# One pool of six places for x and the weight blocks, and a last product stored by quarters

## The chip, the cores and the metric

The kernel runs on one core of one Trainium2 chip. The metric is the device time of one execution in microseconds (us); shown is the median of three runs. A core has five engines that work side by side, each through its own instruction queue in order: PE (TensorE, matrix products; PEld is its loading of weights), DVE (VectorE), ACT (ScalarE), POOL (GpSimd) and SP (SyncE, which here only issues DMA transfers). Products end up in PSUM, eight banks of 128 partitions by 512 float32 values; everything else lies in SBUF or in DRAM.

## The reference, cut to what matters

```
kv  = einsum('bhsd,bhse->bhde', k, v)            # 8 batches, 8 heads, 576 rows, 64 features
o   = einsum('bhsd,bhde->bhse', q, kv)
x   = o / sqrt(mean(o*o, -1) + 1e-6) * g_norm    # laid out as 4608 tokens x 512
h   = x @ w_in                                    # 512 x 2048
g   = max(h, 0)**2
out = g @ w_out                                   # 2048 x 512, all float32
```

## The kernel before, in words

**Strips.** The 4608 tokens are 36 tiles of 128; four tiles make a strip, so there are nine strips, 0 to 8. Per strip the kernel does the "up" products (x times `w_in`), squares the positive part into four quarters `gt`, then does the "down" products (`gt` times `w_out`). Attention for the next strip is cut into small slices (`slices`, L675 to L740) that are put between the steps of the current strip.

**Products by Strassen's scheme.** A product of 2 by 2 blocks is made of seven block products, numbered 1 to 7 in the code (`p`). Strip 0 uses plain products up and one level of the scheme down. Strip 1 uses one level up and two levels down. Strips 2 to 8 use two levels both ways: each block product p is again seven small products, called j. In `small_products` (L1043) one j is four matmuls in the code and eight PE instructions in the profile. `together` (L1058) adds the small products of one p from PSUM into an output tile: one ACT copy and five DVE additions.

**Weight blocks.** The weights of one deep down product come as two blocks: block (s, p, 0) is 768 KB from `w_out` and holds j = 3, 1, 2; block (s, p, 1) is 1024 KB from `w_deep` and holds j = 5, 6, 7, 4. A deep up product takes one 768 KB block from `w_in_deep`. All are asked for in one fixed order (`to_stream`, L912) by calls of `stream` (L921). Such a call takes a place in a pool and issues a DMA on SP; if the place is still being read, the DMA instruction waits on SP, and all that is queued on SP behind it waits too. The pool ("stream", L1345) has four places of 8 KB per partition. In strips 0 and 1 the same places also hold tiles of computed weights: `w_t` (sums of `w_out` blocks, made on DVE and stored to `w_deep`) and `w_i` (sums of `w_in`, made on POOL in `deep_sums_in`, L1146, and stored to `w_in_deep`).

**x.** A strip's x, transposed, lies in a tile `xT` of 8 KB per partition, in a pool of its own with two places (L86). It is opened by the first of `open_xt` (L622). Tiles 0 to 8 are transposed on PE and copied in by ACT (`first_features`, `features`). Later tiles are transposed on DVE (`squares_x`), stored to DRAM (`send_x`, L646) and read back by four DMAs of 64 KB (`fetch_x`, L651). The read-back is asked for when a planner's clock, which adds 2.2 per up step of strip 1 and 3.2 per down step, has gone on by 18 for tiles 9 to 11, or by 6 for later tiles.

**Order around the change.** Strip 1 has 28 up steps (i = 0 to 27), then 14 down steps: k = 0 to 6 through `DEEP_ORDER` = (4, 1, 2, 6, 5, 7, 3), each in two halves i = 0, 1. At each up step i of strip 1 one slice of attention is done, slice i - 1 of the list from L702 on. Blocks are asked for at up steps 17, 20, 21 and 23, and then by `down_deep` (L1084) after the products of each half, up to k = 6, i = 0. In strips 2 to 8, k = 0 has no products of i = 0 left (they are done among the up steps), and i = 1 asks for two.

**The last product.** In strip 8 the last product is p = 3 (k = 6). Its j come in three groups, (1), (2, 6, 5, 7), (4, 3), and `together` does one part of the sums after each; the last part ends with one DMA of 256 KB (`send`, L946). Products 5 and 3 share their PSUM banks: 3 adds on top of 5.

Of the kernel before, what the change touches and what calls it, by code (L numbers as in the profile page):

```python
# [10 lines left out]
FP32 = mybir.dt.float32  # L11
# [4 lines left out]
ALU = mybir.AluOpType  # L16
# [4 lines left out]
def kernel(  # L21
# [35 lines left out]
    P = 128  # L57
# [25 lines left out]
    rest_pool = ctx.enter_context(tc.tile_pool(name="rest", bufs=1))  # L83
    qt_pool = ctx.enter_context(tc.tile_pool(name="qt", bufs=NP + 1))
    xn_pool = ctx.enter_context(tc.tile_pool(name="xn", bufs=3))
    xt_pool = ctx.enter_context(tc.tile_pool(name="xt", bufs=2))  # L86
    small = ctx.enter_context(tc.tile_pool(name="small", bufs=3))
    g_pool = ctx.enter_context(tc.tile_pool(name="g", bufs=4))
    dram = ctx.enter_context(tc.tile_pool(name="dram", bufs=1, space=bass.MemoryType.DRAM))
    c_pool = ctx.enter_context(tc.tile_pool(name="c", bufs=6))  # L90
    conv = ExitStack()
    raw_pool = conv.enter_context(tc.tile_pool(name="raw", bufs=8))
    spare_pool = conv.enter_context(tc.tile_pool(name="spare", bufs=1))
    wtmp = conv.enter_context(tc.tile_pool(name="wtmp", bufs=4))
# [526 lines left out]

    def open_xt(s):  # L622
        if s not in xt:
            xt[s] = xt_pool.tile([P, STRIP // SQ, NP, SQ], FP32, name="xT", tag="xT")
        return xt[s]

    def features(n):
# [18 lines left out]
    def send_x(n):  # L646
        d = sent[n] = dram.tile([P, 4, NP, SQ], FP32, name="x_d", tag="x_d", bufs=2 * NT)
        nc.sync.dma_start(out=d, in_=squared.pop(n))
        tiles_due.append((clock[0] + (6 if n >= DEEP_UP * NT + NT else 18), fetch_x, (n,)))

    def fetch_x(n):  # L651
        s, i = divmod(n, NT)
# [47 lines left out]
    ready[1] = len(slices)  # L700
    T, K, last = transposed_query, key_value, query_pairs(1)[2]
    slices += [(query_means, (last,)), (K, (2, 0, 1)), (T, (2, 0)), (roots_normalized, (last,)), (T, (2, 1))]  # L702
    slices += [(T, (2, 2)), (features, (last[0],)), (T, (2, 3)), (K, (2, 2, 3))]
    pair_ends = []
    for b in range(2, B):
        pairs = query_pairs(b)
# [93 lines left out]
    def out_rows(n):  # L800

        to = []
        for t in range(2):
            m, c = divmod(n + t, PAIR)
            b, c_b = (2 * m, c) if c < C else (2 * m + 1, c - C - 1)
            if c == C:
                for h in range(2):
                    rows = out[(2 * m + h) * S + C * P : (2 * m + h + 1) * S, :]
                    to.append((slice(REST * h, REST * (h + 1)), slice(t, t + 1), rows.rearrange("p (t e) -> p t e", t=1)))
                continue  # L810
            if t and c_b > 0:
                continue
            cs = slice(c_b, c_b + (1 if t or c_b == C - 1 else 2))
            both = slice(t, t + cs.stop - cs.start)
            rows = out[b * S : b * S + C * P, :].rearrange("(sp c) e -> sp c e" if b < Q_ON_PE else "(c sp) e -> sp c e", c=C)
            to.append((slice(0, P), both, rows[:, cs]))
        return to
# [125 lines left out]
    def out_tile():  # L943
        return c_pool.tile([P, 2, DH], FP32, name="o_sb", tag="c")

    def send(s, th, eh, o):  # L946
        for i, (part, t, rows) in enumerate(out_rows(NT * s + 2 * th)):
            eng = nc.scalar if i % 2 and s == N_STRIP - 1 and (th, eh) == (0, 1) else nc.sync
            eng.dma_start(out=rows[:, :, ts(eh, DH)], in_=o[part, t, :])

    def store_deep_sums(p, w):
        if p in (6, 4):
# [84 lines left out]

    PLACE = {1: (0, 0), 2: (0, 1), 6: (0, 2), 5: (1, 0), 7: (1, 1), 3: (1, 2), 4: (1, 3)}

    LAST_PLACE = {1: (1, 0), 2: (0, 0), 6: (0, 1), 5: (0, 2), 7: (0, 3), 3: (1, 1), 4: (1, 2)}  # L1040
    place = lambda s, p: LAST_PLACE if s == N_STRIP - 1 and p in (5, 3) else PLACE

    def small_products(s, p, js):  # L1043
        c = "B" if p in (4, 2, 5, 3) else "A"
        if js[0] == 1 and p not in (6, 7, 3):
            opened[c] = set()
            chain[c] = [fpsum.tile([P, 4, P], FP32, name=f"ps_{c}", tag="f") for _ in range(2)]
        for j in js:
            x, i = place(s, p)[j]
            a, w = leaf[p][j], w_blk.pop((s, p, j))  # L1050
            for f in range(FQ // 2):
                nc.tensor.matmul(  # L1052
                    chain[c][x][:, i, :], lhsT=a[:, f, :], rhs=w[:, f, :],
                    start=x not in opened[c] and f == 0, stop=f == FQ // 2 - 1, skip_group_check=True,
                )
            opened[c].add(x)

    def together(s, p):  # L1058

        def small(j, n=1):  # L1060
            x, i = place(s, p)[j]
            return chain["B" if p in (4, 2, 5, 3) else "A"][x][:, i : i + n]

        o = part[p] = out_tile()
        q = o.rearrange("p t (h e) -> p (t h) e", h=2)
        one = lambda t: t.to_broadcast([P, 2, P])
        add = lambda out, a, b: nc.vector.tensor_tensor(out=out, in0=a, in1=b, op=ALU.add)  # L1067
        yield nc.scalar.copy(q[:, 3:4], small(1))  # L1068
        add(q[:, 1:3], one(q[:, 3:4]), small(2, 2))
        add(q[:, 0:4:3], one(q[:, 2:3]), small(5, 2))  # L1070
        add(q[:, 2:3], q[:, 3:4], small(5))

        if p == 3:
            add(o, o, part[6])
        yield
        add(q[:, 0:4:3], q[:, 0:4:3], small(3, 2))
        if p == 3:
            send(s, 0, 1, o)
        for a, th, eh in {2: [(1, 0, 0)], 7: [(4, 1, 0), (5, 1, 1)]}.get(p, []):
            add(part[a], part[a], o)  # L1080
            send(s, th, eh, part[a])
        yield

    def down_deep(s, k, i):  # L1084
        p = DEEP_ORDER[k]
        if s == N_STRIP - 1 and k == 6 and i == 1:

            steps = together(s, p)
            for js in ((1,), (2, 6, 5, 7), (4, 3)):
                small_products(s, p, js)  # L1090
                next(steps)
            return
        if k == 0 and s >= DEEP_UP:
            if i == 0:
                return
            for j in (7, 5, 6, 3):
                small_products(s, p, (j,))
            stream(2)
            deque(leaf_next[1], 0)
            for slot in sorted(relus):  # L1100
                relu_squares(slot)
            for slot in sorted(first_s):
                add_s1(s, slot)
            return
        if k == 6 and i == 1:
            small_products(s, p, (4,))
            return
        if s < N_STRIP - 1 or k < 6:
            small_products(s, p, ((1, 2, 3), (4, 5, 6, 7))[i])
        stream()  # L1110
        q11, q12, q21, q22 = (gq[s, q] for q in (11, 12, 21, 22))
        if i == 1:
            if k == 0:
                nc.vector.tensor_tensor(out=q12, in0=q12, in1=q22, op=ALU.add)
            if k == 3:
                minus(nc.vector, q22, q22, q11)
            if k == 4:
                minus(nc.vector, q21, q21, q11)
            if k == 6:
                deque(together(s, p), 0)  # L1120
            return
        if k == 2:
            minus(nc.vector, q11, q12, q11)
        if k == 3:
            leaf_sums(s, DEEP_ORDER[k + 1])
        if k:
            deque(together(s, DEEP_ORDER[k - 1]), 0)
        if k < 6 and k != 3:
            leaf_sums(s, DEEP_ORDER[k + 1])
        if k == 6 and s + 1 < N_STRIP:  # L1130
            leaf_x(s + 1, 0)
            sum_x(s + 1, 5)
            sum_x(s + 1, 6)
            leaf_x(s + 1, 1)
# [163 lines left out]
    for s in range(N_STRIP):  # L1298
# [25 lines left out]
        for i, (w, fn, a) in enumerate(steps):  # L1324
            if s == 0 and i < n_up:

                if 4 <= i < 10:
                    convert(3 + i)
                if i == 0:
                    load_next()  # L1330
                    load_rest(1, nc.sync)
                    load_next()
                if i == 1:
                    load_next()
                if i == 2:
                    for b in range(2):
                        load_q_rest(b, nc.sync)
                if i == 14:
                    for b in range(2):
                        store_first(b)  # L1340
            elif s == 0 and i == n_up:
                convert(len(conversions))
                conv.close()

                stream_pool = ctx.enter_context(tc.tile_pool(name="stream", bufs=4, reuse_waits="tile"))  # L1345
                sum_pool = ctx.enter_context(tc.tile_pool(name="sum", bufs=8, reuse_waits="tile"))
            if s == 0 and n_up <= i < n_up + 2:
                for g in range(2 * (i - n_up), 2 * (i - n_up) + 2):
# [9 lines left out]
            if s:  # L1358
# [26 lines left out]
                    stream()  # L1385
                continue
            if i == n_up:
                stream(2)
            if i in (n_up + 8, n_up + 11):
                load(2, (i - n_up) // 11, nc.sync, "q")  # L1390
            if i == n_up + 12:
# [5 lines left out]
            n = i + 1 - (n_up - 6)  # L1397
            pairs, m = divmod(max(n - 2 * NP, 0), 3)
            attend(min(ready[0] + min(max(n, 0), 2 * NP) + (n >= 2 * NP) + 4 * pairs + (0, 2, 2)[m], goal))
            if i == n_up + 6:  # L1400
                stream()
            while deep_due and i not in (n_up + 1, n_up + 4, n_up + 12, n_up + 13):
                deque(store_deep_sums(*deep_due.popleft()), 0)
            if i == n_up + 2:
# [39 lines left out]
```

## Time and profile before

| | us |
|---|---|
| median of three runs (891.94 to 893.4) | 892.87 |
| the profiled execution, its own time | 889.28 |
| span of its instructions in the profile | 887.3 |
| PE busy in the span | 876.6 |
| PE waiting for other engines, in all | 6.8 |
| DVE, ACT, POOL busy | 721.4, 352.3, 307.3 |

Span and own time are of one profiled execution, which lasted 3.6 us less than the median of the runs without a profile. "Busy" is time in which at least one instruction of the engine is under way. A list of waits names, for an engine and a line, who was waited for, then us in total, times, and the longest. A timeline line gives start, duration, engine, line, operation, tiles written and read, count, and in brackets the idle time before it. The chain of waits follows the work that ended last back to its causes. DMA to landing is the time from the issue of a transfer to its completion.

### The profile page before, as it was taken

Reading aid. Unit: us, or ns where it says so; the run is one execution under the profiler, and the core shown is the slowest. Engines: PE = TensorE matmul, PEld = TensorE weight load, DVE = VectorE, ACT = ScalarE, POOL = GpSimd, SP = SyncE. Lnnn points to the kernel's source line nnn. Section 1 sums busy time; section 2 is a strip of 40 time slices with the busy share of each in tenths; the row PEclk is TensorE's granted clock in tenths of the full one; section 3 lists DMA queues with packets and bytes.
Section 4 is the critical chain, followed back from the end, with each engine's and each line's share of the span. In section 5 each row is a group of like instructions: output and inputs, shape, how many; then the busy total and the mean of one; then the engine's idle time right before and its main releaser. Section 6 shows DMA issues by size and latency. Waiting matters only on the chain.

```text
span 887.3 us, 20876 instructions
## 1 busy us (share of the span) xinstructions
PE 876.6 (99%) x8296; PEld 821.8 (93%) x8296; DVE 721.4 (81%) x1233; ACT 352.3 (40%) x806; POOL 307.3 (35%) x315
## 2 busy tenths in 40 slices
PE   8999999999999999999999999999999999999998
PEld 7445888889999999999999999999999999999998
DVE  4999998879768986798678966897888778876886
ACT  4898242320048303740365034902491147102710
POOL 0000005610558223731474045604470447044700
PEclk9999999999999999999999999999999999999999
DMA  9998997989999888979887988898658864884385
GB/s 314 315 316 251 304 366 234 273 305 328 327 232 262 297 309 249 237 269 331 238 222 250 321 268 247 251 307 285 211 166 309 297 181 171 309 291 155 137 313 180
DMA packets 169953, 235.73 MB, mean 266 GB/s; under 512 B 79488, under 2 KB 134272, under 8 KB 161536
## 3 DMA queue, kind: packets, MB, share of 16 engines
q1 hardware_dynamic: 169696, 234.40, 82.3%
q8 instruction: 65, 1.06, 0.5%
q14 instruction: 32, 0.26, 0.1%
q10 hardware_dynamic: 160, 0.00, 0.0%
HBM read 197.66 MB, written 36.70 MB: 264 GB/s over the span
## 4 chain that ended last, share of the span: by engine, by line
PE 82%; DVE 10%; DMA 3%; ACT 3%; issue 2%; SPq 0%; POOL 0%; DVEq 0%; POOLq 0%; ACTq 0%
PE ps_B L1052 22%; PE ps_A L1248 19%; PE ps_A L1052 16%; PE ps_B L1248 9%; PE ps_C L1248 5%; PE ps_A L835 4%; PE kv_ps L432 2%; PE x_ps L468 2%; DVE w_c L269 2%; PE ps_B L835 1%; DMA w_deep<-w_t 1%; DVE w_t L289 1%; DVE wt L289 1%; PE ps_C L835 1%; DVE w_c L263 1%
## 5 line engine op out<-in xcount | busy, mean ns | idle before, releaser
L1052 PE MATMUL ps_B<-w_blk,g_s 128*128 128x128 f32 x1024 | 126.1, 275 | 0.0
L1052 PEld LDWEIGHTS ps_B<-w_blk,g_s 128*128 128x128 f32 x1024 | 120.0, 192 | 0.1
L1248 PE MATMUL ps_A<-x_l,w_in 128*128 128x128 f32 x784 | 103.8, 275 | 0.3 <-ACT snap L1265 0.3
L1052 PE MATMUL ps_B<-w_blk,gt 128*128 128x128 f32 x768 | 97.5, 275 | 1.5 <-DMA w_blk<-w_out 1.5
L289 POOL TENSOR_TENSOR x_l<-xT 128x256 f32<-128x256 f32 x21 | 15.4, 734 | 238.6 <-PE ps_A L1052 187.9
L1248 PEld LDWEIGHTS ps_A<-x_l,w_in 128*128 128x128 f32 x784 | 95.4, 192 | 0.6 <-ACT snap L1265 0.5
L1052 PE MATMUL ps_A<-w_blk,g_s 128*128 128x128 f32 x768 | 93.6, 275 | 0.0
L1052 PEld LDWEIGHTS ps_B<-w_blk,gt 128*128 128x128 f32 x768 | 91.5, 192 | 1.7 <-DMA w_blk<-w_out 1.7
L1052 PEld LDWEIGHTS ps_A<-w_blk,g_s 128*128 128x128 f32 x768 | 89.6, 192 | 0.0
L1260 POOL TENSOR_TENSOR snap<-snap,gt 128x512 f32<-128x512 f32 x35 | 45.9, 1310 | 119.2 <-ACT snap L1265 103.7
L1265 ACT COPY snap<-ps_A 128x512 f32<-128x512 f32 x63 | 36.9, 585 | 109.5 <-PE ps_A L1248 96.2
L1198 ACT ACTIVATE gt<-gt 128x512 f32<-128x512 f32 x112 | 70.1, 626 | 12.8 <-DVE gt L1260 12.6
L1052 PE MATMUL ps_A<-w_blk,gt 128*128 128x128 f32 x576 | 72.2, 275 | 0.0
L1199 ACT ACTIVATE gt<-gt 128x512 f32<-128x512 f32 x112 | 70.7, 631 | 3.6
L1052 PEld LDWEIGHTS ps_A<-w_blk,gt 128*128 128x128 f32 x576 | 68.2, 192 | 0.0
L1067 DVE TENSOR_TENSOR o_sb<-o_sb,ps_B 128x256 f32<-128x256 f32 (+1 forms) x128 | 49.4, 386 | 19.2 <-ACT o_sb L1068 11.8
L1068 ACT COPY o_sb<-ps_A 128x128 f32<-128x128 f32 x24 | 6.4, 265 | 145.7 <-PE ps_A L1052 145.7
L1154 POOL TENSOR_TENSOR w_i<-w_in 128x512 f32<-128x512 f32 x7 | 10.7, 1524 | 148.1 <-DMA q<-in_q_dram 140.8
L289 DVE TENSOR_TENSOR gt<-gt 128x2048 f32<-128x2048 f32 (+1 forms) x29 | 59.7, 2063 | 0.0
L1260 POOL TENSOR_TENSOR gt<-gt,snap 128x512 f32<-128x512 f32 x42 | 52.4, 1277 | 17.6 <-DVE snap L1260 17.4
L1248 PE MATMUL ps_B<-x_l,w_blk 128*128 128x128 f32 x392 | 52.1, 276 | 0.0
L1248 PE MATMUL ps_A<-x_l,w_blk 128*128 128x128 f32 x392 | 51.9, 275 | 0.0
(183 smaller groups left out, 1835.0 us busy)
## 6 DMA issues: line engine op xcount, KB each, us to landing
w_blk<-w_deep SPq DMA_DIRECT2D x56, 1024.0 KB, 6.5
w_blk<-w_out SPq DMA_DIRECT2D x56, 768.0 KB, 6.0
w_blk<-w_in_deep SPq DMA_DIRECT2D x49, 768.0 KB, 5.5
raw<-in_moe_w_in_dram SPq DMA_DIRECT2D x16, 512.0 KB, 7.0
raw<-in_moe_w_out_dram SPq DMA_DIRECT2D x16, 512.0 KB, 5.8
k<-in_k_dram SPq DMA_DIRECT2D x29, 256.0 KB, 5.2
v<-in_v_dram SPq DMA_DIRECT2D x29, 256.0 KB, 5.4
x_d<-x_q SPq DMA_DIRECT2D x27, 256.0 KB, 5.4
```

What stands on the lines that cost most here:

```text
L269: yield nc.vector.scalar_tensor_tensor(out=ci, in0=high, scalar=-(2**30), in1=ci, op0=ALU.bitwise_and, op1=ALU.bitwise_or)
L289: eng.tensor_tensor(out=out, in0=a, in1=b, op=ALU.subtract)
L432: nc.tensor.matmul(ps[ts(h, D), i], lhsT=a, rhs=w, start=i == 0 and c == 0, stop=c == C, skip_group_check=True)
L468: nc.tensor.matmul(ps[half, r, i, ts(p, D)], lhsT=q[row, half], rhs=kvd[b, p][row, row], start=True, stop=True)
L835: nc.tensor.matmul(bank[BANK[p]][:, i, :], lhsT=lhsT(k), rhs=rhs(k), start=p in (1, 5, 2) and i == 0 and k == 0, stop=k == n - 1, skip_gro ...
L1052: nc.tensor.matmul(chain[c][x][:, i, :], lhsT=a[:, f, :], rhs=w[:, f, :], start=x not in opened[c] and f == 0, stop=f == FQ // 2 - 1, skip ...
L1067: add = lambda out, a, b: nc.vector.tensor_tensor(out=out, in0=a, in1=b, op=ALU.add)
L1198: nc.scalar.activation(o, o, AF.Relu)
L1199: nc.scalar.activation(o, o, AF.Square)
L1248: nc.tensor.matmul(ps[:, i, :], lhsT=w, rhs=rhs, start=j in (1, 2, 5) and i == 0, stop=True, skip_group_check=True)
L1260: add = lambda eng, out, a, b: eng.tensor_tensor(out=out, in0=a, in1=b, op=ALU.add)
L1265: nc.scalar.copy(t, ps)
```

## The change

- The pool of x with two places goes. Strip 0's x lies in a pool with one place that is given up, with the pools of the weight conversion, at the end of strip 0's up products. From strip 1 on a strip's x takes a place in the stream pool, which has six places instead of four. Strip 1's x is opened before the first two blocks are asked for.
- In strip 0's down products the fourth block is asked for at step `n_up + 4` (product 5, first half) instead of `n_up + 6` (product 6, first half).
- In every deep strip, blocks are asked for one call sooner: one `stream()` more at the start of k = 0, none at k = 6.
- The read-back of tiles 9 to 11 is due 12 after the store, not 18.
- Slice order: the DVE transpose of query pair (2, 3) goes ahead of `features` of tile 8.
- The last product: products 5 and 3 of strip 8 get five PSUM banks (three of them from attention's pool) instead of two, so that j = 1; 2, 6; 5, 7; 4; 3 each have a bank of their own. The groups become (1), (2, 6), (5, 7), (4), (3). DVE does all sums, starting from product 6's sums plus j = 1, and each quarter of the tile (128 by 128, 64 KB) is sent when it is complete: three on SP, the last on ACT's queue. Product 5 of strip 8 adds j = 4 and j = 3 in two additions instead of one.

```
-    xt_pool = ctx.enter_context(tc.tile_pool(name="xt", bufs=2))
+    xt_pool = conv.enter_context(tc.tile_pool(name="xt", bufs=1))
...
+            if s == 0:
+                xt[s] = xt_pool.tile([P, STRIP // SQ, NP, SQ], FP32, name="xT", tag="xT")
+            else:
+                t = stream_pool.tile([P, 4, FQ // 2, P], FP32, name="xT", tag="w_blk")
...
-        tiles_due.append((clock[0] + (6 if n >= DEEP_UP * NT + NT else 18), fetch_x, (n,)))
+        tiles_due.append((clock[0] + (6 if n >= DEEP_UP * NT + NT else 12), fetch_x, (n,)))
...
-    slices += [(T, (2, 2)), (features, (last[0],)), (T, (2, 3)), (K, (2, 2, 3))]
+    slices += [(T, (2, 2)), (T, (2, 3)), (features, (last[0],)), (K, (2, 2, 3))]
...
+    def send_quarter(s, th, eh, o, t, h, eng):
+        for part, at, rows in out_rows(NT * s + 2 * th):
+            if at.start <= t < at.stop:
+                eng.dma_start(
+                    out=rows[:, t - at.start, eh * DH + h * P : eh * DH + (h + 1) * P], in_=o[part, t, ts(h, P)]
+                )
...
-    LAST_PLACE = {1: (1, 0), 2: (0, 0), 6: (0, 1), 5: (0, 2), 7: (0, 3), 3: (1, 1), 4: (1, 2)}
+    LAST_PLACE = {1: (0, 0), 2: (1, 0), 6: (1, 1), 5: (2, 0), 7: (2, 1), 4: (3, 0), 3: (4, 0)}
...
+            if s == N_STRIP - 1 and p == 5:
+                two = apsum.tile([P, 2, 4, P], FP32, name="ps_last", tag="x", bufs=1)
+                chain[c] += [two[:, 0], two[:, 1], apsum.tile([P, 4, P], FP32, name="ps_last", tag="at")]
...
+        if s == N_STRIP - 1 and p == 5:
+            for j, i in ((4, 3), (3, 0)):
+                add(q[:, i], q[:, i], small(j)[:, 0])
+            return
...
+        if k == i == 0:
+            stream()
         if s == N_STRIP - 1 and k == 6 and i == 1:
-            steps = together(s, p)
-            for js in ((1,), (2, 6, 5, 7), (4, 3)):
+            sums = {
+                1: [(slice(0, 4), 1)], 6: [(slice(1, 2), 2), (slice(2, 4), 6), (slice(0, 1), 6)],
+                7: [(slice(2, 3), 5), (slice(2, 3), 7), (slice(0, 1), 5), (slice(3, 4), 7)],
+                4: [(slice(3, 4), 4)], 3: [(slice(0, 1), 3)],
+            }
+            for js in ((1,), (2, 6), (5, 7), (4,), (3,)):
                 small_products(s, p, js)
-                next(steps)
+                for to, j in sums[js[-1]]:
+                    n = to.stop - to.start
+                    nc.vector.tensor_tensor(
+                        out=q[:, to], in0=rest if j == 1 else q[:, to], in1=at[j].to_broadcast([P, n, P]), op=ALU.add
+                    )
+                    if (j, to.start) in ((2, 1), (7, 2), (4, 3), (3, 0)):
+                        eng = nc.scalar if j == 3 else nc.sync
+                        send_quarter(s, 0, 1, o, *divmod(to.start, 2), eng)
...
-        stream()
+        if k < 6:
+            stream()
...
-                stream_pool = ctx.enter_context(tc.tile_pool(name="stream", bufs=4, reuse_waits="tile"))
+                stream_pool = ctx.enter_context(tc.tile_pool(name="stream", bufs=6, reuse_waits="tile"))
...
             if i == n_up:
+                open_xt(1)
                 stream(2)
+            if i == n_up + 4:
+                stream()
...
-            if i == n_up + 6:
-                stream()
```

More of the change, by code (lines that the diff above doesn't have):

```diff
@@ L623, in open_xt @@
         if s not in xt:
-            xt[s] = xt_pool.tile([P, STRIP // SQ, NP, SQ], FP32, name="xT", tag="xT")
+            if s == 0:
+                xt[s] = xt_pool.tile([P, STRIP // SQ, NP, SQ], FP32, name="xT", tag="xT")
+            else:
+                t = stream_pool.tile([P, 4, FQ // 2, P], FP32, name="xT", tag="w_blk")
+                xt[s] = t.rearrange("p n f e -> p (n f e)").rearrange("p (a q t) -> p a q t", q=NP, t=SQ)
         return xt[s]
@@ L946, in send @@
     def send(s, th, eh, o):
-        for i, (part, t, rows) in enumerate(out_rows(NT * s + 2 * th)):
-            eng = nc.scalar if i % 2 and s == N_STRIP - 1 and (th, eh) == (0, 1) else nc.sync
-            eng.dma_start(out=rows[:, :, ts(eh, DH)], in_=o[part, t, :])
+        for part, t, rows in out_rows(NT * s + 2 * th):
+            nc.sync.dma_start(out=rows[:, :, ts(eh, DH)], in_=o[part, t, :])
+    def send_quarter(s, th, eh, o, t, h, eng):
[4 more added lines that the diff above has]
+                )
     def store_deep_sums(p, w):
@@ L1085, in down_deep @@
         p = DEEP_ORDER[k]
+        if k == i == 0:
+            stream()
         if s == N_STRIP - 1 and k == 6 and i == 1:
-            steps = together(s, p)
-            for js in ((1,), (2, 6, 5, 7), (4, 3)):
-                small_products(s, p, js)
-                next(steps)
+            o = out_tile()
+            q, rest = (t.rearrange("p t (h e) -> p (t h) e", h=2) for t in (o, part[6]))
+            at = {j: chain["B"][x][:, i : i + 1] for j, (x, i) in place(s, p).items()}
+            sums = {
[4 more added lines that the diff above has]
+            for js in ((1,), (2, 6), (5, 7), (4,), (3,)):
+                small_products(s, p, js)
+                for to, j in sums[js[-1]]:
[6 more added lines that the diff above has]
+                        send_quarter(s, 0, 1, o, *divmod(to.start, 2), eng)
             return
```

## The prediction

> **What bounds the kernel now.** I read the page's busy times first, then PE's list of waits, the timelines of SP and PE around its longest wait, and the chain of waits at the end.
>
> ```profile
> PE 876.6 (99%) x8296; PEld 821.8 (93%) x8296; DVE 721.4 (81%) x1233; ACT 352.3 (40%) x806; POOL 307.3 (35%) x315
> ```
>
> PE's waits (us in total, times, longest):
>
> ```profile
> PE ps_B L1052 <- DMA w_blk<-w_out: 1.5, 1, 1.5
> ...
> PE ps_A L835 <- DVE o_sb L1001: 0.4, 1, 0.4
> ...
> PE xt_ps L632 <- DVE x_n L563: 0.3, 1, 0.3
> ```
>
> PE is busy for 876.6 of 887.3 us. Outside that lie 10.7 us: waits of 6.8 (three of them shown) and 3.8 after the last matmul. No matmul goes or changes shape, so nothing beyond these 10.7 us can be won. Strips 3 to 8 show no wait for a block. SP's timeline, then PE's:
>
> ```profile
> 186.31 0.84 SPq L933 DMA_DIRECT2D w_blk<-w_out  x1
> 199.04 0.32 SPq L939 DMA_DIRECT2D w_blk<-w_deep  x1
> 199.46 0.38 SPq L648 DMA_DIRECT2D x_d<-x_q  x1
> 199.88 5.53 SPq L655 DMA_DIRECT2D xT<-x_d  x8
> 205.45 0.43 SPq L933 DMA_DIRECT2D w_blk<-w_out  x1
> ```
>
> ```profile
> 210.33 2.05 PE L1052 MATMUL ps_B<-w_blk,gt 128*128 128x128 f32 x16 [1.50 <-DMA w_blk<-w_out]
> ```
>
> Here is the 1.5 us. SP stands still from 187.2 to 199.04: the next block, (1, 1, 1), got the place of (1, 4, 0), which PE reads until 199.02. Behind it are queued the store of tile 11, eight read-backs of tiles 9 and 10 (5.53 us of issuing), and only then block (1, 2, 0), issued at 205.45. It lands 4.8 us later, at 210.3; PE wanted it at 208.83.
>
> The end, from the chain of waits; then the last store in the timeline, and the stores of the last 17 us in the DMA view (KB each, us to landing):
>
> ```profile
> 881.78 0.43 DVE o_sb L1067
> ...
> 883.01 0.70 DVE o_sb L1067
> ...
> 883.80 0.42 DVE o_sb L1067
> ```
>
> ```profile
> 884.30 0.37 SPq L949 DMA_DIRECT2D out_dram<-o_sb  x1
> ```
>
> ```profile
> out_dram<-o_sb SPq DMA_DIRECT2D x3, 256.0 KB, 2.2
> ```
>
> The last matmul ends at 883.46, but DVE is busy with the full-width addition until 883.71; the last sum ends at 884.22, the store is issued at 884.30 and lands 2.2 us later (886.5); the span closes 0.8 after that.
>
> **What the Trainium skill says.** "DMA: Bandwidth & Descriptors", Issuing engines are not separate DMA queues: transfers of SP and ACT share 16 engines, a second issuer saves issue time only. No store of before is issued by ACT, so the trace doesn't show it. Same page, Queues, rings and completion order: each engine takes descriptors in ring order. The trace agrees: block (1, 1, 0), issued at 186.31 behind 1 MB and other traffic, lands after 11.8 us, while (1, 1, 1), issued at 199.04 into an idle ring, needs 5.3. "PSUM — Partial Sum Buffer", PSUM bank collisions raise a hardware error: guard PSUM by bank. In the tail before, j = 2, 6, 5, 7 share a bank and DVE starts only after all four (881.78, PE's last of them at 881.68), as that asks.
>
> **Part 1, the shared pool and block (1, 2, 0).** Two waits end. With the read-back due after 12, tile 9 (stored at up step 16, clock 37.4) comes due at step 22 instead of 25, and tile 10 at 23 instead of 26: ahead of block (1, 1, 1), in the time when SP stood still. The eight DMAs then go at about 187 to 193 (before, 5.53 us for eight). Block (1, 1, 1) needs a place. Occupied are two x and four blocks or `w_i` tiles; strip 1's x is read last by PE at 194.4, so it or the old `w_i` place serves from 194.4, and at worst again (1, 4, 0)'s at 199.0. Block (1, 2, 0) is now asked for at the start of k = 0 and follows the store of tile 11 at once: 199.5 at the latest instead of 205.45. Plus even 6.8 (the landing of its neighbour (1, 2, 1)) that is 206.3, before 208.8. The 1.5 us go. Bounds: 0, if the wait only moves, to 1.5.
>
> What is late next? From 204 to 245 the 16 DMA engines are 0.95 to 1.08 busy, and from issue times and landings blocks reach PE with 0.2 (block (1, 2, 1)), 2.0, 0.9, 1.3, 1.2, 2.6, 1.5, 1.3 and 0.4 us to spare. PE running up to 2.2 us earlier would eat these, were it not that the supply moves too: from 195 to 200 the DMA engines are only 0.32 busy (3.4 us idle), and the read-backs, (1, 1, 1) and tile 11's store move into that time; also each block is asked for a half product (2.7 to 3.6 us) sooner. I take the full 1.5.
>
> **Part 2, DVE in strips 0 and 1.** At 128.59 DVE waits 0.46 for the store of an earlier `w_t` tile, whose place the next one takes; DVE has no other gap near, so the sum at 131.13 that PE waits for (0.42) is late by that. With x(1), blocks 6 and 7 and two `w_t` there are six places, and the block of product 6 (free at 120.5) or another is there for this tile. PE's 0.42 goes: 131.35 is before PE's 131.45. Bounds 0 to 0.42; taken: 0.42. The fourth block goes out some 2.5 us sooner (before 120.68, needed at 131.9 anyway), ahead of the `w_t` store at 118.13, whose landing nobody now waits for: 0.
>
> The slice order: `features` of tile 8 comes one up product (1.73 us) later, so its 0.29 us wait on DVE is covered: -0.29. In exchange the transpose of query (2, 3) stands in DVE's queue at 159.5 while its DMA lands at about 162.0. DVE idles 2.5 us. Behind it wait two sums of `w_t`, one squared-positive step and then the four `w_deep` stores on SP (163.89). DVE waited 2.86 for PE at 166.22, which takes the delay up on DVE; SP's queue is up to 2 us late until 188. Block (1, 4, 1) (185.82, landing 196.3) is wanted at 198.85 less the 0.7 won, 198.1: covered by 1.8. If its landing moves by the full 2.4 it costs 0.6. Bounds of this edit: -0.29 to +0.6; taken: -0.2.
>
> **Part 3, strips 2 to 8.** During the up steps four blocks and two x fill six places, as before. From k = 0 strip s's x is dead (last read at up slot 45 of 55), and the fifth block takes its place; at k = 6 the number is back to four. No request waits for a later release than before, and PE had no block wait to lose. 0; if a place is badly chosen, see the second rival.
>
> **Part 4, the tail.** PE ends j = 1 at 878.11, then 2, 6, 5, 7, 4, 3 at 879.00, 879.89, 880.79, 881.68, 882.57, 883.46 (0.893 each). DVE is busy with product 7's sums until 879.63. Then come one addition of 128x512 (0.69, as the row of that shape out of PSUM) and, after (2, 6), additions of 128x128 (0.287), 128x256 (0.42), 128x128: done at 881.4. After (5, 7), visible at 881.78, four of 128x128: 883.0. One for j = 4: 883.3. One for j = 3 starts 0.1 after PE, at 883.56, and ends at 883.85 instead of 884.22: -0.37. The last store is 64 KB instead of 256. "DMA: Bandwidth & Descriptors", Anatomy of one DMA, gives a fixed part of about 2.0 us plus bytes over 436 GB/s: 0.45 less for 192 KB (an estimate; its fit is for the software path, and its 2.6 for 256 KB is above the 2.2 seen). Nearest rows: 64 KB read-backs land in 1.8 at best; ACT's two issues of `g_col` took 0.58 against SP's 0.37. So 2.2 - 0.45 + 0.2 = 1.95: -0.25. Bounds: ACT's `g_col` landings, up to 3.8 for 0.2 KB in tiny pieces, would make the tail 1.2 worse; 1.75 would make it -0.82. Taken: -0.6. The other quarters are sent by 883.4 and are down by 885.4. Product 5's one addition more (0.15) lies on DVE with 1.3 us of waiting after it: 0.
>
> **Sum.** 1.5 + 0.42 + 0.2 + 0.6 = 2.7 us off the span of 887.3: 884.6. The profiled execution's own time (889.28) would be 886.6, and the median, 3.6 above it, 892.87 - 2.7 = 890.2.
>
> **Rivals.** *The block wait moves.* DMA busy near 1.0 from 204 to 245 speaks for it, with 0.2 and 0.4 us to spare at two blocks; the 3.4 us of idle DMA before speak against it. Then only 0.42 + 0.2 + 0.6 remain: 891.6.
>
> *A place that comes free late (slower).* An x now takes whichever place is free. In each of strips 2 to 8 the first read-back could be given the place of a block that PE still reads; SP would be held for a group of 24 matmuls (2.7 us), and the next block be late by that. It costs only beyond the spare time of the block (2.0 at the better ones): 0.7 in each of seven strips, 4.9 - 2.7 = +2.2: 895.1. It decides from a hold that exceeds the spare time by 0.4 us per strip (2.7/7). For it: six places are exactly filled. Against: a free place exists at each opening by count, and SP already held for PE at most requests without PE noticing.
>
> *The early part doesn't come.* DVE's idle 2.5 us reach PE through block (1, 4, 1) (+0.6 instead of -0.2) and ACT's store eats its gain (-0.37 only): 1.5 + 0.42 - 0.6 + 0.37 = 1.7: 891.2.
>
> **How the numbers follow.** All gains 0.66; block wait moves 0.10; late place 0.14; early part lost 0.10. 0.2% is 1.8 us, about what a measurement of this kernel can tell from no change. The likeliest case (its own range 889.4 to 891.0) is faster; the moved wait lies within; the early loss is half in each; the late place is slower, with 0.01 of the likeliest lost to unforeseen waits. Faster 0.70, same 0.15, slower 0.15. The range runs from 889.1 (every bound at its best: 1.5 + 0.42 + 0.29 + 0.82 = 3.0, with 0.8 for the scatter of the runs) up to 892.9, which takes in the moved wait and the early loss but not the late place.
>
> **What would show it.** Right: PE without a wait at block (1, 2, 0); the eight read-backs issued before block (1, 1, 1); no DVE wait on `w_deep<-w_t`; SP's standstill of 11.9 us filled; the last sum about 0.4 after the last matmul, and a span end near 3.2 after it. Wrong: a PE wait on a `w_blk` landing elsewhere, an ACT or SP wait on a `w_i` or PE release at an x tile, or a last store issued by ACT that needs over 2.5 us.

## The result, and the profile after

Twelve runs of each kernel, side by side: before 892.88 us (891.79 to 894.8), after 893.28 us (891.52 to 895.15), ratio 1.0003 with a 95% interval of 0.9993 to 1.0013. Nothing was won that can be measured; the forecast was 890.2 us, with 892.9 as the upper end of its range. The profiled execution of the changed kernel lasted 892.37 us with a span of 890.5; that of the kernel before had 889.28 and 887.3.

The busy times of after are those of before; no engine has more work:

```profile
PE 877.1 (99%) x8296; PEld 821.6 (92%) x8296; DVE 721.3 (81%) x1239; ACT 352.1 (40%) x805; POOL 306.5 (34%) x315
```

So the time must lie in PE's waits again. The list of waits of PE, after (us in total, times, longest):

```profile
PE xt_ps L636 <- DVE x_n L563: 1.6, 1, 1.6
...
PE ps_A L839 <- DVE o_sb L1011: 1.2, 1, 1.2
PE ps_last L1065 <- DVE o_sb L1119: 1.1, 1, 1.1
...
PE ps_B L880 <- ACT gt L887: 0.8, 1, 0.8
PE ps_A L1065 <- DMA w_blk<-w_deep: 0.8, 1, 0.8
```

The 1.5 us for block (1, 2, 0) are gone, as forecast. In their place stand four waits: 1.6 (none at this place before; the 0.3 of the list before is of the same line, but stood later, at `features` of tile 8) and 1.2 (0.4 before) in strip 0, 0.8 for block (1, 1, 1) in strip 1, and 1.1 in the last product. The fifth that is new, 0.8 for ACT, stands at 56.04, in the up products of strip 0; three of the five profiles with the shared pool are without it, and the argument leaves it aside.

Four places on PE's timeline cut the span into stretches: the start of product 1 of strip 0, the start of product 4 of strip 0 (the sum of part 2 of the prediction is needed there), the first up product of strip 2, and the end of the last matmul. Each number below is the difference of two such points of one profile; the first column is the point itself.

| us | product 1, strip 0, starts | to product 4 | to strip 2 | to the last matmul's end | to the span's end |
|---|---|---|---|---|---|
| before | 83.68 | 48.19 | 107.15 | 644.44 | 3.84 |
| after | 84.80 | 50.77 | 105.94 | 645.68 | 3.31 |
| difference | +1.12 | +2.58 | -1.21 | +1.24 | -0.53 |

The sum is +3.20, which is 890.5 - 887.3. The first column, which holds the wait at 56.04, isn't put down to the change: over the eleven profiles here it lies between 83.5 and 85.9, and in both kinds of kernel near either end. The others are read one by one.

**Strip 0, +2.58.** ACT's timeline, first before, then after: the copy of strip 1's first tiles of x into its place.

```profile
104.64 1.07 ACT L633 COPY xT<-xt_ps 128x512 f32<-128x512 f32 x2 [4.95 <-PE xt_ps L632]
108.53 0.59 ACT L845 COPY snap<-ps_B 128x512 f32<-128x512 f32 x1 [2.82 <-PE ps_B L835]
```

```profile
113.67 1.07 ACT L637 COPY xT<-xt_ps 128x512 f32<-128x512 f32 x2 [13.95 <-DMA w_deep<-w_t]
114.63 0.60 ACT L849 COPY snap<-ps_B 128x512 f32<-128x512 f32 x1
115.11 1.12 ACT L477 ACTIVATE sq<-x_ps 128x512 f32<-128x512 f32 x2
```

ACT stands still for 13.95 us (4.95 before, for PE), because the place it writes to still holds a `w_t` tile whose store has not landed. The chain of waits of after shows that store, and what follows it:

```profile
104.93 8.29 DMA w_deep<-w_t
...
113.67 0.09 ACT xT L637
```

The store was issued at 104.93 and landed at 113.2. Queued on ACT behind the copy are a snapshot of PSUM (108.53 before, 114.63 after) and the squares of the next tile of x. DVE then has no squares to add, stands still for 4.1 us, and PE waits twice for DVE:

```profile
115.77 1.28 DVE L485 TENSOR_REDUCE ms<-sq 128x8 f32<-128x512 f32 x2 [4.12 <-ACT sq L477]
```

```profile
119.36 1.23 PE L636 MATMUL xt_ps<-ident,x_n 128*128 128x128 f32 x8 [1.55 <-DVE x_n L563]
135.57 7.17 PE L839 MATMUL ps_A<-w_blk,gt 128*128 128x256 f32 x32 [1.17 <-DVE o_sb L1011]
```

**Strip 1, -1.21.** SP's timeline, after:

```profile
190.04 0.58 SPq L937 DMA_DIRECT2D w_blk<-w_out  x1
191.85 11.97 SPq L659 DMA_DIRECT2D xT<-x_d  x8
203.92 0.38 SPq L943 DMA_DIRECT2D w_blk<-w_deep  x1
204.40 0.38 SPq L652 DMA_DIRECT2D x_d<-x_q  x1
204.87 0.38 SPq L937 DMA_DIRECT2D w_blk<-w_out  x1
```

The eight read-backs now stand ahead of block (1, 1, 1), in the stretch in which SP stood still before, but issuing them took 11.97 us instead of 5.53. (1, 1, 1) went out at 203.92 (199.04 before), and PE waited 0.77 for it. Block (1, 2, 0), issued at 204.87, landed 6.9 us later, and PE began on it at 212.92, so it came with 1.1 us to spare. By the clock it landed later than before (211.8 against 210.3), since all of this stretch runs later here; counted from the issue of block (1, 1, 0) it went out after 14.8 us instead of 19.1, and that is the gain.

**The last product, +1.24 and -0.53.** The timeline of the end, after: PE, DVE and the store.

```profile
884.07 1.00 DVE L1119 TENSOR_TENSOR o_sb<-o_sb,ps_last 128x128 f32<-128x128 f32 x4 [0.42 <-PE ps_last L1065]
885.13 1.16 PE L1065 MATMUL ps_last<-w_blk,gt 128*128 128x128 f32 x8 [1.10 <-DVE o_sb L1119]
...
887.22 0.29 DVE L1119 TENSOR_TENSOR o_sb<-o_sb,ps_last 128x128 f32<-128x128 f32 x1 [0.61 <-PE ps_last L1065]
887.54 0.35 ACTq L957 DMA_DIRECT2D out_dram<-o_sb  x1
```

PE stops for 1.10 us before j = 4, until DVE has read the sums of j = 5 and 7. Behind the last matmul the end is 0.53 us shorter, as meant, though not by the 0.6 of the forecast.

### The profile page after: what moved, and what is told of

Its sections match the earlier page's. It is cut to its first block, busy times and chain, and to the rows that moved or that the text cites. A ratio compares the mean times of both kernels' runs of the same rounds, so it can differ in the third digit from the quotient of the medians.

```text
span 890.5 us, 20894 instructions
## 1 busy us (share of the span) xinstructions
PE 877.1 (99%) x8296; PEld 821.6 (92%) x8296; DVE 721.3 (81%) x1239; ACT 352.1 (40%) x805; POOL 306.5 (34%) x315
## 4 chain that ended last, share of the span: by engine, by line
PE 79%; DVE 10%; DMA 5%; ACT 2%; issue 2%; POOL 1%; SPq 0%; DVEq 0%; ACTq 0%; POOLq 0%
PE ps_B L1065 21%; PE ps_A L1282 19%; PE ps_A L1065 17%; PE ps_B L1282 9%; PE ps_C L1282 5%; PE ps_A L839 2%; PE kv_ps L432 2%; DVE w_c L269 2%; DMA w_deep<-w_t 2%; PE x_ps L468 2%; DMA w_blk<-w_out 2%; DVE w_t L289 1%; DVE wt L289 1%; DVE w_c L263 1%; PE ps_last L1065 1%
## 5 line engine op out<-in xcount | busy, mean ns | idle before, releaser
L1065 PE MATMUL ps_B<-w_blk,g_s 128*128 128x128 f32 x976 | 120.4, 275 | 0.0
L1065 PEld LDWEIGHTS ps_B<-w_blk,g_s 128*128 128x128 f32 x976 | 114.5, 192 | 0.1
L1065 PE MATMUL ps_B<-w_blk,gt 128*128 128x128 f32 x752 | 95.2, 275 | 0.0
L1065 PEld LDWEIGHTS ps_B<-w_blk,gt 128*128 128x128 f32 x752 | 89.6, 192 | 0.1
L1080 DVE TENSOR_TENSOR o_sb<-o_sb,ps_B 128x256 f32<-128x256 f32 (+1 forms) x121 | 46.8, 387 | 16.5 <-ACT o_sb L1081 11.8
```

The source lines that it names most:

```text
L1065: nc.tensor.matmul(chain[c][x][:, i, :], lhsT=a[:, f, :], rhs=w[:, f, :], start=x not in opened[c] and f == 0, stop=f == FQ // 2 - 1, skip ...
```

## The experiments

**1. Strip 1's x claims its place when it is opened.** The copy waits for a place that `open_xt(1)`, called ahead of all requests for blocks, should have had already. If a place is handed out not at the opening but at the first write, one early write into the tile must end the wait. POOL writes one column, which is later written over:

```
-                open_xt(1)
+                nc.gpsimd.memset(open_xt(1)[:, 0, 0, 0:1], 0.0)
```

> The changed kernel, but one column of strip 1's x tile is written by POOL (a memset of 128x1) where the tile is opened, before the first two blocks are asked for. Theory A (an x tile takes its place at its first write, by then all six places were given to two blocks, three w_t tiles and the third block, so ACT's copy waited for a w_t store to land): the copy that began at 113.67 begins within 1 us of the transposes (about 105.7), PE's wait of 1.6 at xt_ps goes and its 1.2 on o_sb falls below 0.5; the span is 2.2 to 2.6 shorter than the changed kernel's 890.5, but for scatter of the start. Theory B (the late w_t store is a slow landing by chance, not a matter of places): ACT's wait of 8 us or more stays, span as the changed kernel's.

Measured: 889.54 us (887.66 to 891.01), ratio to before 0.9962 (0.9949 to 0.9976). ACT's timeline:

```profile
106.88 1.07 ACT L637 COPY xT<-xt_ps 128x512 f32<-128x512 f32 x2 [6.10 <-PE xt_ps L636]
```

The early write itself ran on POOL long before any `w_t` was made:

```profile
85.25 0.10 POOL L1422 MEMSET xT<- 128x1 f32 x1 [83.05 <-PE ps_C L880]
```

The copy waits for its matmul again and for no store. The stretch to product 4 fell from 50.77 to 47.60 us; PE has neither the 1.6 nor the 1.2. Against the changed kernel, 0.9962 and 1.0003 leave 0.0041, or 3.7 us; their intervals lie apart. This wait is the main reason why the change won nothing. What the claim takes away from the `w_t` tiles comes back small: DVE waits 0.9 us for a `w_deep` store at a `w_t`, which the change was to end.

**2. The read-back due after 18 again, all else as changed.**

```
-        tiles_due.append((clock[0] + (6 if n >= DEEP_UP * NT + NT else 12), fetch_x, (n,)))
+        tiles_due.append((clock[0] + (6 if n >= DEEP_UP * NT + NT else 18), fetch_x, (n,)))
```

> The changed kernel with the read-back of tiles 9 to 11 due after 18 again. Theory A (the eight read-backs each wait for the landing of the transfer eight before, and so hold block (1, 1, 1) until 203.9): block (1, 1, 1) is issued at 194 to 199, before the read-backs, PE's wait of 0.8 for it goes, and (1, 2, 0) still lands in time; 0.8 shorter than the changed kernel. Theory B (the read-backs cost the same wherever they stand): the wait moves to (1, 2, 0) as in the kernel before, 0.5 to 1.5 us; no shorter.

Measured: 893.42 us (891.78 to 895.03), ratio 1.0003 (0.9993 to 1.0014). SP's timeline:

```profile
198.24 0.32 SPq L943 DMA_DIRECT2D w_blk<-w_deep  x1
...
199.09 8.21 SPq L659 DMA_DIRECT2D xT<-x_d  x8
207.40 0.38 SPq L937 DMA_DIRECT2D w_blk<-w_out  x1
```

(1, 1, 1) goes out ahead of the read-backs, PE's wait for it is gone, and (1, 2, 0), asked for after them at 207.40, still comes with less than 0.1 us of waiting. The stretch to strip 2 is 104.97 us against 105.94. So the 0.8 us go with the read-backs' place in SP's queue; but the profile of experiment 1, also with 12, has no wait for (1, 1, 1) either, so they don't come in every execution. In the medians they can't be seen: the intervals of both ratios are 0.001 (0.9 us) wide to each side.

**3 and 4. The new last product alone, and a mended one.** Both are the kernel before with the new last product; the second gives j = 4 a tile from the pool of the other products instead of the second half of the two-bank tile `two`:

```
-                chain[c] += [two[:, 0], two[:, 1], apsum.tile([P, 4, P], FP32, name="ps_last", tag="at")]
+                own = fpsum.tile([P, 4, P], FP32, name="ps_own", tag="f")
+                chain[c] += [two[:, 0], own, apsum.tile([P, 4, P], FP32, name="ps_last", tag="at")]
```

> The kernel before with only the new end of the last product. Theory A (j = 4 lies in one two-bank tile with j = 5 and 7, and PE's first write of j = 4 waits until DVE has read them): PE waits 1.0 to 1.2 for DVE before j = 4; from the last matmul to the end of the span 3.3 instead of 3.8; in all 0.5 to 0.7 slower than before. Theory B (the wait comes from DVE being late in the changed kernel's strip 8): no such wait, 0.5 faster than before.

> As e3_tail_alone, but j = 4 gets a PSUM bank of its own from the pool of five (a tile of its own). Theory A: PE doesn't wait in the last product, the last sum ends 0.4 after the last matmul, 3.3 from the last matmul to the end of the span: 0.5 faster than before. Theory B (PE waits for DVE whatever the tiles, because DVE's four additions after j = 7 come too late): a wait of about 1 us stays.

Measured: 892.79 us (891.1 to 894.47), ratio 0.9999 (0.9988 to 1.0011), for the new last product as it is; 891.87 us (890.23 to 893.3), ratio 0.999 (0.998 to 1.0), with j = 4 in a tile of its own. The first has the wait of PE, in its list of waits; the second has none in the last product:

```profile
PE ps_last L1061 <- DVE o_sb L1113: 1.1, 1, 1.1
```

So the hold before j = 4 goes with the tile it shares with j = 5 and 7, though it has a bank of its own. (The mend also takes the bank from another pool; two tiles in the same pool weren't tried.) Mended, the last product may be worth the forecast 0.6 us or a little more (-0.9, from 0 to -1.8); as it was made it is worth nothing.

**5 and 6. Both mends, and the read-back after 12 or 18.** The changed kernel with the claim of 1 and the tile of 4; the second also has the 18 of 2.

> The changed kernel with two mends: strip 1's x claims its place by a write of one column on POOL when it is opened, and j = 4's sums of the last product lie in a tile of their own. Theory A (the two losses are independent, and each is the wait that the trace names): the claim alone gave 889.5, the mended tail takes PE's last wait of 1.1 us away, so 888.4 (887.9 to 888.9), ratio to before 0.995; no PE wait at ps_last, the span closes 3.0 after the last matmul. Theory B (the tail's wait only ran beside the drain that follows anyhow): as the claim alone, 889.5, ratio 0.996.

> As the kernel with claim and mended tail, and the read-back of x due after 18 up steps as before. Theory A (the earlier read-back only moves the wait from block (1, 2, 0) to (1, 1, 1); the sooner request for the fifth block is what frees (1, 2, 0)): no block wait over 0.3 us in strip 1, time equal to or up to 0.8 us below the one with 12. Theory B (the earlier read-back is needed): block (1, 2, 0) waits 1 to 2 us again and the time is 1 to 2 us above the one with 12.

Measured: 887.6 us (887.38 to 888.14), ratio 0.9946 (0.9933 to 0.9958), and 887.43 us (886.44 to 888.06), ratio 0.9943 (0.9928 to 0.9957). Both beat both kernels, by about 5 us. The ratios of 1 and 5 differ by 0.0016, or 1.4 us, where 1.1 was expected of the mended last product; their intervals overlap, so the times alone don't show it. The profiles do: PE's wait is gone, and the stretch to the last matmul's end is 644.3 us instead of 645.7 (table below). So theory A of the first run holds for the wait, though 887.6 lies just below its range and the span closes 3.3, not 3.0, after the last matmul. The end of the first one's timeline, with PE running through:

```profile
880.51 1.06 PE L1066 MATMUL ps_own<-w_blk,gt 128*128 128x128 f32 x8
880.71 1.00 DVE L1120 TENSOR_TENSOR o_sb<-o_sb,ps_last 128x128 f32<-128x128 f32 x4 [0.42 <-PE ps_last L1066]
881.40 1.06 PE L1066 MATMUL ps_last<-w_blk,g_s 128*128 128x128 f32 x8
```

Between 12 and 18 no difference is seen in the times (0.2 us). The profiles differ as in 2: with 12, PE waits 0.66 for (1, 1, 1); with 18, for no block in strip 1. For the sum in strip 0, PE waits 0.80 in the first profile and not at all in the second.

**7 and 9. The kernel before, with 12 for 18 alone.** Is the earlier read-back, without the pool and the earlier requests, enough for block (1, 2, 0)? The edit is that of 2 in the other direction.

> The kernel before with one number changed: the read-back of x due after 12 up steps instead of 18. Theory A (Part 1 of the prediction, the read-backs alone stood between block (1, 1, 1) and (1, 2, 0)): no PE wait for block (1, 2, 0), or one below 0.5; 1.5 to 2.5 us faster than before, ratio 0.998. Theory B (the eight read-backs, each waiting for the landing of the transfer eight before it, now hold block (1, 1, 1) up, and the wait moves): PE waits 0.8 or more for (1, 1, 1), and the time is within 0.8 us of before, ratio 0.9995.

Measured: 890.67 us (887.52 to 892.49), ratio 0.9974 (0.9963 to 0.9984), or -2.3 us. The time speaks for theory A, its profile for B, since PE waited in it 1.39 for (1, 1, 1) and 1.14 for a later block:

```profile
208.22 1.16 PE L1052 MATMUL ps_A<-w_blk,gt 128*128 128x128 f32 x8 [1.39 <-DMA w_blk<-w_deep]
241.32 1.16 PE L1052 MATMUL ps_B<-w_blk,gt 128*128 128x128 f32 x8 [1.14 <-DMA w_blk<-w_deep]
```

The profiled execution took 892.45 us, nearly the slowest of the twenty. So the same kernel was profiled again:

> The kernel before with the read-back due after 12, once more, for a second profile: the first profile was of an execution of 892.45 us, slower than all but one of its twenty runs, and showed waits of 1.4 for block (1, 1, 1) and 1.1 for a block at 241. Theory A (these waits are not typical; with the read-backs gone ahead, block (1, 2, 0) has no wait and (1, 1, 1) at most a small one): own time 889 to 891, block waits in strip 1 below 1.0 in all, and the stretch from product 4 of strip 0 to the first up product of strip 2 lasts 105.5 to 107 us (107.2, 107.8, 108.4 and 109.8 in four profiles with the read-back after 18). Theory B (the wait for (1, 1, 1) is always there, and the gain lies elsewhere): 1.0 us or more for (1, 1, 1) again, stretch above 107.5.

Measured: 887.8 us (889 to 891 was expected), span 885.8, with the kernel before at 890.6 beside it. No PE wait for a block of strip 1 appears among its waits, and the stretch to strip 2 lasts 105.52 us. SP's timeline:

```profile
188.58 9.99 SPq L655 DMA_DIRECT2D xT<-x_d  x8
199.24 0.82 SPq L939 DMA_DIRECT2D w_blk<-w_deep  x1
```

(1, 1, 1) went out at 199.24 here and at 202.50 in the first profile: whether the read-backs hold it up long enough to be felt differs from execution to execution. Theory A holds for the time; the wait of theory B is real but not in every execution.

**8. The kernel before, unchanged, profiled again.** The profiles of 3 and 4, whose kernels are those of before up to the last product, show larger waits in strips 0 and 1 than the profile that the prediction read.

> The kernel before, unchanged, for a second profile. Theory A (its first profile was an execution with smaller waits than most): span 889 to 891; in strip 0, PE waits 1.2 to 2.1 for the sum of DVE that was late by 0.42 in the first profile, and DVE 1.1 to 2.1 for the place of w_t (0.46 in the first); for blocks of strip 1 PE waits 1.7 to 3.7 (1.5 in the first). Theory B (the first profile was typical, and the losses in the other profiles come from their changed tails): o_sb wait 0.4, block wait 1.5, span 887.3.

Measured: 891.63 us, span 889.6. Of theory A the span and the block waits came (1.63 for (1, 2, 0) and 0.89 for a later one, 2.5 together); the wait for the sum in strip 0 did not, though DVE waited 0.9 at `w_t`.

```profile
211.46 2.05 PE L1052 MATMUL ps_B<-w_blk,gt 128*128 128x128 f32 x16 [1.63 <-DMA w_blk<-w_out]
240.30 1.16 PE L1052 MATMUL ps_B<-w_blk,gt 128*128 128x128 f32 x8 [0.89 <-DMA w_blk<-w_deep]
```

The profiles together, in the stretches of the first table:

| us | to product 4 | to strip 2 | to the last matmul's end | to the span's end |
|---|---|---|---|---|
| before | 48.2 | 107.2 | 644.4 | 3.8 |
| before, again | 47.7 | 108.4 | 644.5 | 3.8 |
| before with the new last product | 49.0 | 107.8 | 645.7 | 3.0 |
| before with the mended one | 49.9 | 109.8 | 645.0 | 3.0 |
| before, 12 (first, second) | 49.2, 47.8 | 108.9, 105.5 | 644.3, 644.4 | 3.9, 3.8 |
| after | 50.8 | 105.9 | 645.7 | 3.3 |
| after, 18 | 52.5 | 105.0 | 645.7 | 3.3 |
| after, claim | 47.6 | 105.2 | 645.7 | 3.3 |
| after, claim, mended | 48.6 | 105.8 | 644.3 | 3.3 |
| after, claim, mended, 18 | 47.6 | 105.1 | 644.3 | 3.3 |

Each column tells one story. To product 4: 47.6 when nobody waits, up to 49.9 where DVE waits for the place of `w_t`, 50.8 and 52.5 where ACT waits for the place of x. To strip 2: 105.0 to 105.5 without a block wait, 107.2 to 109.8 for the kernel before. To the last matmul: 645.7 wherever j = 4 shares the tile, 644.3 where it doesn't (of the 645.0 of one profile, 0.2 is a wait for a block of a later strip; the rest isn't explained).

## Why the prediction was wrong

**Part 2 failed, and with it the forecast.** Its sentence "With x(1), blocks 6 and 7 and two `w_t` there are six places, and the block of product 6 (free at 120.5) or another is there for this tile" counted x(1) among the holders from its opening on. Experiment 1 shows that it held nothing then: with an early write into x the wait goes, so a place goes to a tile at its first write. By the order of the code (no view shows the places) the two blocks, the third block and the `w_t` tiles came first, and x, written at 104.6 before, had to take a place whose `w_t` store landed at 113.2. The prediction had the opposite order, so it looked for the late tile among the `w_t`, and there DVE's wait did end as it said. Taken: -0.42. Measured: +2.58 in the profiles, and 3.7 us between the kernels with and without the claim.

**The rival "a place that comes free late" had the mechanism.** An x tile was given a place in use and held up all that was queued behind it. The prediction put it at the read-backs on SP in strips 2 to 8, seven times 0.7 us. There it didn't come: part 3's zero stands, since the stretch from strip 2 to the last matmul is 644.3 us with the shared pool as without it. It came once, on ACT, in strip 0, where the rival wasn't looked for, although the list of what would show the prediction wrong named an ACT wait at an x tile (for a `w_i` or for PE; it was a `w_t` store).

**Part 1 was right in its effect and wrong in one term.** The wait for (1, 2, 0) went. "The eight DMAs then go at about 187 to 193 (before, 5.53 us for eight)" took the duration of a calm moment into a busy one. SP's list of waits between 185 and 212 us, after, tells what the read-backs waited for:

```profile
SPq L659 <- DMA w_blk<-w_out: 3.8, 2, 2.6
SPq L659 <- DMA x_d<-x_q: 3.2, 1, 3.2
SPq L659 <- DMA w_blk<-w_deep: 2.3, 1, 2.3
SPq L659 <- DMA v<-in_v_dram: 1.7, 2, 1.3
SPq L659 <- DMA w_in_deep<-w_i: 1.6, 1, 1.6
SPq L659 <- DMA k<-in_k_dram: 1.3, 2, 0.8
```

Apart from `x_d`, the data that they read, these are the transfers issued just before them: two blocks from `w_out`, one from `w_deep`, two k, two v, one `w_i` store, eight in all. The last read-back went at 203.52, as the block (1, 1, 0), eight transfers before it, landed (190.04 + 13.46). I read this as a program that goes round eight completion semaphores for SP's transfers, each issue waiting until the one eight before it has landed. That fits what the Trainium skill says in "DMA: Bandwidth & Descriptors", Anatomy of one DMA: a wait for a semaphore is held by the engine that issues the transfer, before it is sent off; here SP needed 11.97 us for the eight issues. The count of eight is inferred from who was waited for, and no run changed it. With landings of up to 13.5 us in a busy stretch, eight issues last as long as those landings. In this profile it cost 0.8 us at (1, 1, 1), where the prediction had nothing: the rival "the block wait moves", in half its size. The rival "the early part doesn't come" fell on both counts: block (1, 4, 1) has no wait, and the store on ACT's queue cost less than assumed.

**The size of parts 1 and 2 was read from one execution.** 889.28 us, the execution profiled before, is below each of the other runs of the kernel before shown here (890.18 at the least). Its block wait of 1.5 and sum wait of 0.42 are near the low end: 1.5, 2.5, 1.9 and 3.7 us for blocks in strip 1, and 0.42, 0, 1.27 and 2.06 for the sum, in the four profiles with the read-back after 18 and separate pools; 2.4 and 0.9 on the mean, where the prediction took 1.5 and 0.42. That the claim brings 3.3 us although it still has the tail's 1.1 fits this: 2.4 + 0.9 = 3.3 at most, plus 0.5 at the end, less the tail's 1.1. It leaves 0.6 us that the terms don't explain, less than the interval of the ratio. The prediction saw that the execution was 3.6 us below the median and put the difference into a constant; part of it lay in the very waits it was pricing.

**Either half of part 1 would have done.** The earlier read-back alone brings 2.3 us (7, 9); the pool with the earlier requests does as well with 18 as with 12 (5, 6). The prediction credited both together, which is right for the wait and says nothing on which is needed.

**The slice order came as worked out.** DVE waits at the transpose of query (2, 3), 2.33 us where 2.5 was forecast, and PE doesn't feel it:

```profile
165.54 0.71 DVE L384 STREAM_TRANSPOSE qT<-q 128x512 f32<-128x512 f32 x1 [2.33 <-DMA q<-in_q_dram]
```

PE's wait of 0.29 at `features` of tile 8 is gone from its list. The gain of 0.2 was too small to be measured by itself; no run had this part alone.

**Part 4 failed in its first sentence.** "PE ends j = 1 at 878.11, then 2, 6, 5, 7, 4, 3 at 879.00, 879.89, 880.79, 881.68, 882.57, 883.46 (0.893 each)" took PE's pace from the kernel before and priced only DVE behind it. It read the five banks as five free places; but j = 4 lies in one tile with 5 and 7, and PE waited 1.10 for DVE. The rest was near: the last sum 0.03 us after the last matmul, in 0.29, and the store on ACT's queue landed after 1.6 us where 1.95 was estimated:

```profile
out_dram<-o_sb SPq DMA_DIRECT2D x3, 64.0 KB, 1.5
out_dram<-o_sb ACTq DMA_DIRECT2D x1, 64.0 KB, 1.6
```

From the landing to the end of the span it then takes 1.36 us (890.5 - 889.14) where it took 0.8 before; why isn't known. Net, -0.6 became +0.7 (1.24 - 0.53).

**Sum.** In ratios to before: 1.0003 as the change was made, 0.9962 with the claim, 0.9946 with the tile for j = 4 as well. The first step is 3.7 us, the second 1.4; that these add up is no proof, since they are differences of the same three ratios, and the second rests on the profiles. With both waits gone the gain is 4.8 us, where 2.7 was forecast. So the gains were there, and two new waits, both from storage that was handed out otherwise than the prediction took it, ate them. Of the signs named for being right all came in the profile after: no wait at block (1, 2, 0), the read-backs ahead, no DVE wait for a `w_t` store, the last sum 0.3 us and the end 3.3 after the last matmul. They watched the waits that were to go; the wait of PE for DVE in the last product was in neither list of signs.

## What to carry to other kernels

When tiles of different kinds share a pool, write down who holds each place at every first write, not at every opening, and look at what stands in the queue of the engine that makes that first write; an early write of one column was worth 3.7 us here. Give each part that is to be read early a tile of its own, since a bank of its own didn't keep PE from waiting here. And before a wait of 1 us is priced, see a second execution: the waits that one profile shows may be less than half of what they are in another.

## What the runs showed that was not expected

- Eight transfers in flight seem to be the limit on SP's queue in this program (inferred from who was waited for): eight issues of 64 KB took 5.5 to 5.8 us in a calm stretch, and 6.8 to 12.1 us where the transfers before them needed up to 13.5 us to land.
- A store of 64 KB landed 1.5 us after its issue on SP's queue and 1.6 on ACT's, one of 256 KB 2.2: 0.6 to 0.7 us for 192 KB, where an estimate from the fit for the software path in the Trainium skill ("DMA: Bandwidth & Descriptors", Anatomy of one DMA) gave 0.45.
- The time of one kernel scatters widely: 890.18 to 896.15 us in 25 runs of before, 887.52 to 892.49 in the twenty of experiment 7. With both mends five runs lie within 0.8 us (with 18: 1.6). That the waits which the mends take away also make the times scatter is likely by this, but five runs don't show it.
